# The output projection's last twelve token blocks: seven block products in place of eight, with their sums on GpSimd

## The chip, the cores and the metric

The kernel runs on one core of a Trainium2 chip. The metric is device time in microseconds (us) of one execution; smaller is better. The engines are TensorE (PE, matmuls; PEld is its weight load), VectorE (DVE), ScalarE (ACT), GpSimd (POOL) and SyncE (SP), which here only issues DMA transfers. Each engine works its own queue strictly in program order, so an instruction that waits holds up all that stands behind it on its engine.

## What is computed

A gated mix of two attention blocks over 2048 tokens of width 1024, in float32. Block A is linear attention, block B is softmax attention with 32 heads of width 32; each has its own input projection and output projection:

```python
def reference(A_x, A_wqkv, A_wo, B_x, B_wqkv, B_wo, gate_w):
    x = A_x
    g = _sigmoid((x * gate_w).sum(-1, keepdims=True))
    a = _A_ref(x, A_wqkv, A_wo)        # linear attention, ... @ wo
    b = _B_ref(x, B_wqkv, B_wo)        # softmax attention, o.reshape(B, S, D) @ wo
    return g * a + (1 - g) * b
```

The change touches only the last product, `o @ wo` of block B (2048x1024 by 1024x1024), and what mixes it into the result.

## The kernel before, in words

A float32 product at full speed is made of three matmuls: each operand is written as hi + lo (`split`, L252: ACT rounds the source to fp32r as hi, then DVE or POOL subtracts hi from the source to get lo), and `three` (L144) adds hi·hi, hi·lo and lo·hi in one PSUM bank. The order of all instructions is fixed in Python: a planner keeps a modelled time per engine (`T`, `use`) and picks streams until the attention heads are done. From then on, in `output` (L1252), the order is the plain order of the code.

The output stage goes over 16 blocks of 128 tokens in the order `t_order` (L1157). For a block n:

- `load_o` (L1172) and `load_all` (L1178) fetch it into one tile of the ring `o_ring`: the left half takes the attention output from DRAM, transposed (L1175, k parts 0 to 6, 448 KB; L1188 and L1193 the last k part), the right half takes `ra` (L1176, 512 KB), block A's result for these tokens. A tile is fetched again when the block that used it is done.
- `split_o` (L1195) splits the attention output of a whole block: one ACT cast and one DVE subtraction of 128x1024, into one of four tiles `xo_t`.
- `gate` (L1211) computes g and 1-g from x (two DVE products of 128x512 with a sum, a chain of small DVE and ACT steps) and scales `ra` by g on ACT (L1225); then `load_g` fetches x for the block after next.
- `out_pe` (L1230) runs three matmuls of 128x512 per k part and column half: 8 parts, 2 halves, 48 matmuls per block.
- `out_done` (L1241) evicts a bank on DVE: `ra` becomes (1-g) · bank + `ra` (L1246); then SP stores 256 KB to `out` (L1247).

Blocks 0 and 1 have only their last k part left when the final loop (L1286) begins. PSUM has eight banks, and a block holds two. The loop splits and gates block n+1 ahead of the matmuls of block n, so that PE has a block's time in hand. The weights `wo_t` (hi and lo of 1024x1024) stay in SBUF throughout. POOL has nothing to do in this stage.

The lines that matter elsewhere: `pair_ops` (L379) is an earlier stage in which POOL forms sums of weight tiles (L387 to L392) while DVE runs the subtractions of `split` (L254); L1093 is POOL's running sum in the attention heads, beside which DVE adds to a PSUM bank (L1102).

## Time and profile before

| what | value |
|---|---|
| median of three runs | 2846.59 us (2845.34 to 2848.77) |
| the profiled execution | 2848.47 us, its span 2846.7 us |
| PE busy, share of the span | 2835.8 us, 100% |
| DVE, ACT, POOL busy | 2237.9, 1618.4, 1855.0 us |
| chain that ended last | PE 98%, DMA 1%, DVE 1% |

The profile takes one execution; its span runs from the first to the last instruction, and 1.8 us of the measured time lie around it. Read first the chain that ended last: it names the engine whose work sets the end. Then read the stage in question by itself, since the shares over the whole span mix stages with different limits: the output loop is the last 155 us, and there DVE, ACT and the DMA queues look different from the page's averages. Waits of an engine that is not in the chain cost nothing as long as its results come in time.

### The profile page before, as it was taken

The page shows a single profiled execution, that of the slowest core. Times are in us where ns is not written, and L with a number is a line of the kernel's source. Part 1 is how long each engine was busy: PE and PEld are TensorE (multiplying, and loading weights), DVE is VectorE, ACT ScalarE, POOL GpSimd, SP SyncE. Part 2 cuts the span into 40 slices and gives each one's busy share as a digit, 9 for nine tenths or more (in the row PEclk, how much of TensorE's full clock was granted, in tenths as well). Part 3 has the DMA queues.
Part 4 walks back from the last instruction along what each step waited for, and adds up shares of the span by engine and source line. Part 5 has one row for each costly group of instructions (what it writes and reads, how often), then busy time and mean ns, then how long its engine had stood idle before and what let it go on. Part 6 is the DMA issues. An engine that isn't in the chain of part 4 may idle for free.

```text
span 2846.7 us, 44413 instructions
## 1 busy us (share of the span) xinstructions
PE 2835.8 (100%) x15744; PEld 2034.0 (71%) x15744; DVE 2237.9 (79%) x3775; ACT 1618.4 (57%) x3007; POOL 1855.0 (65%) x646
## 2 busy tenths in 40 slices
PE   9999999999999999999999999999999999999999
PEld 8888888666666666666666767676766666666787
DVE  6666656888888888888888888888988888886743
ACT  5334320666666667666666666675656656666421
POOL 1212220778898889988988888678778787885000
PEclk9999999999999999999999999999999999999999
DMA  5956865432333224233323334564464354424663
GB/s 168 297 167 209 261 193 166 121 97 90 111 90 93 90 80 117 91 103 94 115 83 94 93 119 149 180 219 141 145 191 146 121 148 132 142 88 139 228 216 102
DMA packets 302498, 400.57 MB, mean 141 GB/s; under 512 B 92682, under 2 KB 185354, under 8 KB 299146
## 3 DMA queue, kind: packets, MB, share of 16 engines
q1 hardware_dynamic: 302276, 397.73, 45.1%
q8 instruction: 124, 2.03, 0.3%
q14 instruction: 98, 0.80, 0.1%
HBM read 287.57 MB, written 108.79 MB: 139 GB/s over the span
## 4 chain that ended last, share of the span: by engine, by line
PE 98%; DMA 1%; DVE 1%; ACT 0%; issue 0%; SPq 0%; ACTq 0%
PE bank L1041 17%; PE bank L890 16%; PE bank L1140 15%; PE bank L147 11%; PE bank L149 11%; PE bank L148 11%; PE bank L410 4%; PE bank L408 4%; PE bank L409 4%; PE bank L943 1%; PE bank L447 1%; PE bank L448 1%; PE bank L449 1%; PE bank L693 1%; DMA big<-xs 0%; PE bank L587 0%
## 5 line engine op out<-in xcount | busy, mean ns | idle before, releaser
L1093 POOL TENSOR_TENSOR big<-big,big 128x1536 f32<-128x1536 f32 (+1 forms) x434 | 1557.6, 3589 | 185.1 <-ACT big L1045 162.6
L895 DVE TENSOR_REDUCE mx<-bank 128x1 f32<-128x512 f32 x2048 | 1310.9, 680 | 314.6 <-PE bank L890 310.4
L1045 ACT ACTIVATE big<-bank 128x512 f32<-128x512 f32 x2048 | 1181.7, 602 | 517.7 <-PE bank L1041 450.3
L1041 PE MATMUL bank<-big,big 128*128 128x512 f32 x2048 | 809.7, 397 | 2.5 <-DMA big<-ml 2.4
L890 PE MATMUL bank<-big,big 128*128 128x512 f32 x2048 | 802.7, 392 | 0.3 <-ACT big L1045 0.3
L147 PE MATMUL bank<-big,big 128*128 128x512 f32 x1408 | 551.9, 392 | 1.9 <-DMA big<-xs 1.9
L149 PE MATMUL bank<-big,big 128*128 128x512 f32 x1408 | 550.3, 391 | 0.4 <-DMA big<-xs 0.4
L148 PE MATMUL bank<-big,big 128*128 128x512 f32 x1408 | 550.4, 391 | 0.0
L1041 PEld LDWEIGHTS bank<-big,big 128*128 128x128 f32 x2048 | 383.9, 188 | 158.9 <-issue 64.8
L1140 PE MATMUL bank<-big,mid 128*32 128x512 f32 x4096 | 459.2, 593 | 0.0
L890 PEld LDWEIGHTS bank<-big,big 128*128 128x128 f32 x2048 | 384.6, 188 | 84.8 <-ACT big L1045 4.6
L1140 PEld LDWEIGHTS bank<-big,mid 128*32 128x32 f32 x4096 | 127.7, 110 | 263.7 <-issue 263.7
L147 PEld LDWEIGHTS bank<-big,big 128*128 128x128 f32 x1408 | 264.4, 188 | 65.3 <-ACT big L1045 5.9
L149 PEld LDWEIGHTS bank<-big,big 128*128 128x128 f32 x1408 | 264.4, 188 | 57.1 <-DMA big<-xs 0.9
L148 PEld LDWEIGHTS bank<-big,big 128*128 128x128 f32 x1408 | 264.4, 188 | 55.2
L1102 DVE TENSOR_TENSOR bank<-bank,big 128x512 f32<-128x512 f32 (+1 forms) x434 | 280.4, 646 | 6.9 <-ACT big L1045 5.3
L1089 POOL TENSOR_TENSOR big<-big,big 128x1536 f32<-128x1536 f32 (+1 forms) x31 | 111.6, 3601 | 235.1 <-ACT big L1045 122.1
L254 DVE TENSOR_TENSOR big<-mid,big 128x512 fp32r<-128x512 f32 x216 | 152.9, 731 | 81.1 <-ACT big L253 80.9
L387 POOL TENSOR_TENSOR mid<-mid,mid 128x512 f32<-128x512 f32 x16 | 20.6, 1289 | 277.1 <-DVE big L254 251.2
L253 ACT CAST big<-mid 128x512 fp32r<-128x512 f32 x216 | 130.1, 624 | 93.1 <-POOL mid L388 53.9
L409 PE MATMUL bank<-big,big 128*128 128x512 f32 x448 | 174.3, 389 | 0.0
L410 PE MATMUL bank<-big,big 128*128 128x512 f32 x448 | 174.3, 389 | 0.0
(103 smaller groups left out, 1977.2 us busy)
## 6 DMA issues: line engine op xcount, KB each, us to landing
big<-xs SPq DMA_DIRECT2D x208, 512.0 KB
qk<-mid SPq DMA_DIRECT2D x128, 256.0 KB
big<-oA SPq DMA_DIRECT2D x64, 512.0 KB
big<-qk SPq DMA_DIRECT2D x96, 256.0 KB
big<-qk SPq DMA_DIRECT2D x384, 64.0 KB
mid<-in_b_wqkv SPq DMA_DIRECT2D x88, 256.0 KB
xs<-big SPq DMA_DIRECT2D x64, 256.0 KB
oA<-mid SPq DMA_DIRECT2D x64, 256.0 KB
```

The costliest lines, as they stand in the source:

```text
L147: yield nc.tensor.matmul(ps, sh, mh_, start=(kt == 0), stop=False)
L148: yield nc.tensor.matmul(ps, sh, ml_, start=False, stop=False)
L149: yield nc.tensor.matmul(ps, sl, mh_, start=False, stop=(kt == NK - 1))
L409: nc.tensor.matmul(ps, sh, ml_, start=False, stop=False)
L410: nc.tensor.matmul(ps, sl, mh_, start=False, stop=(i == HK - 1))
L890: nc.tensor.matmul(bank[b], q[:, t * P:(t + 1) * P], k[:, j * C:(j + 1) * C], start=True, stop=True)
L895: nc.vector.tensor_reduce(m[:, t, j:j + 1], bank[b], AX.X, ALU.max)
L1041: nc.tensor.matmul(bank[b], k[:, t * P:(t + 1) * P], q[:, j * C:(j + 1) * C], start=True, stop=True)
L1045: nc.scalar.activation(pr_t[i][:, j * C:(j + 1) * C], bank[b], AF.Exp, scale=SCALE)
L1093: nc.gpsimd.tensor_add(lacc[:, :qp], lacc[:, :qp], pr(t)[:, :qp])
L1102: nc.vector.tensor_add(lacc[:, qp:] if t == NT - 1 else l_b[:, :n], l_b[:, :n], src)
L1140: nc.tensor.matmul(av_b[j * DH:(j + 1) * DH, :], v[:, t, :], pr(t)[:, j * C:(j + 1) * C], start=(t == 0), stop=(t == NT - 1))
```

## The change

The first four blocks stay as they were. The last twelve are taken in six pairs. A pair's 256x1024 attention output and the 1024x1024 weights are both cut into 2x2 quarters, and the eight quarter products (12 matmuls each, 96 for a pair) are replaced by seven products of sums of quarters (Strassen's scheme), 84 matmuls in all. What is added:

- `t_load`, `t_sums`, `t_part`: `wo` is fetched a second time, in 16 tiles of 256 KB (four k rows i, four tiles each); for each i POOL forms four sums or differences in place (128x512) and three of them are split at once (ACT cast, DVE subtraction); the fourth is split after block 2. They stand between the splits and gates of blocks 0 to 3.
- `operand`: the seven stationary operands of a pair. POOL forms four sums in the ring tiles and also the lo parts of operands 2 to 5; ACT casts all seven; DVE subtracts for operands 0, 1 and 6. Operand i of the next pair is queued after product i of this one.
- `pair`: seven products over four banks. Product 0 stays in its bank; product 2 is added to it, then product 4, and the partial sums are evicted after each step: eight evictions for a pair in place of four. The next pair's blocks are fetched by `load_all` when a pair is done, both at once; the ring has four tiles in place of five.

```diff
-        o_ring.extend(pr_t[slot(H - 1, t)] for t in (NT - 5, NT - 3, NT - 2, NT - 1))
+        o_ring.extend(pr_t[slot(H - 1, t)] for t in (NT - 5, NT - 3, NT - 2))
...
+    def t_load(i):
+        for which, (k, c) in enumerate(((i, 0), (i, 1), (HK + i, 0), (HK + i, 1))):
+            nc.sync.dma_start(t_raw(which, i), b_wo[k * P:(k + 1) * P, c * C:(c + 1) * C])
+
+    def t_part(which, i, raw):
+        hi, lo = t_w[which]
+        split(hi[:, i * C:(i + 1) * C], lo[:, i * C:(i + 1) * C], raw, nc.vector)
...
+    def t_sums(i):
+        b11, b12, b21, b22 = [t_raw(w, i) for w in range(4)]
+        nc.gpsimd.tensor_sub(b11, b12, b11)
+        nc.gpsimd.tensor_sub(b12, b22, b12)
+        nc.gpsimd.tensor_sub(b22, b22, b11)
+        nc.gpsimd.tensor_sub(b21, b21, b22)
+        for which, raw in ((0, b11), (2, b12), (1, b22)):
+            t_part(which, i, raw)
+        if i + 2 < HK:
+            t_load(i + 2)
...
+    def operand(p, i):
...
+        src = (a[0], a[1], a[0], s1, a[2], a[1], a[3])[i]
+        if i == 1:
+            nc.gpsimd.tensor_add(s1, a[2], a[3])
+            nc.gpsimd.tensor_sub(a[2], a[0], a[2])
+        elif i == 2:
+            nc.gpsimd.tensor_sub(a[0], s1, a[0])
+            nc.gpsimd.tensor_sub(a[1], a[1], a[0])
+        eng = nc.gpsimd if 2 <= i < 6 else nc.vector
+        split(op_part(p, i, 0), op_part(p, i, 1), src, eng)
...
+    def pair(p):
...
+        plan = ((0, weights[0], True, (0,)), (1, weights[1], True, (0,)), (0, sums[1], False, (1,)),
+                (2, sums[0], True, (3,)), (0, sums[2], False, (2, 3)), (2, weights[2], False, (1,)),
+                (3, sums[3], True, (2,)))
+        for i, (at, w, first, outs) in enumerate(plan):
+            b = banks[at]
...
+            for k in range(HK):
+                for j, (x_, m) in enumerate(((hi, w[k][0]), (hi, w[k][1]), (lo, w[k][0]))):
+                    nc.tensor.matmul(bank[b], x_[:, sl], m, start=(first and k == 0 and j == 0),
+                                     stop=(k == HK - 1 and j == 2), skip_group_check=not first)
...
+            for o in outs:
...
+                nc.vector.scalar_tensor_tensor(ras[t][:, sl], bank[b], omg_sb[:, tok:tok + 1], ras[t][:, sl],
+                                               op0=ALU.mult, op1=ALU.add)
+                if (o, i) in ((0, 1), (3, 4), (1, 5), (2, 6)):
+                    nc.sync.dma_start(out[tok * P:(tok + 1) * P, sl], ras[t][:, sl])
...
+            if p + 1 < NPAIR_O:
+                operand(p + 1, i)
+            if i == 0:
+                gate(n + 1)
+            elif i == 4 and n + 2 < NT:
+                gate(n + 2)
+        o_done[0] += 2
+        load_all()
...
-        for n in range(NT):
-            if 2 < n + 1 < NT and n >= NF:
+        t_load(0)
+        t_load(1)
+        t_sums(0)
+        for n in range(PAIR_FROM):
+            if n == NF:
                 split_o(n + 1, slice(0, NK))
-            if NF <= n + 1 < NT:
+            if NF <= n + 1:
                 gate(n + 1)
+            if n + 1 < HK:
+                t_sums(n + 1)
             for c in range(NQC):
                 for k in range(NK - 1 if n < NF else 0, NK):
                     out_pe(n, c, k)
+                if n == PAIR_FROM - 1:
+                    for i in range(2):
+                        operand(0, 2 * c + i)
                 out_done(n, c)
+            if n == NF:
+                for i in range(HK):
+                    t_part(3, i, t_raw(2, i))
+        for i in range(4, 7):
+            operand(0, i)
+        for p in range(NPAIR_O):
+            pair(p)
```

DVE's queue from block 2's split (into big5) to block 3's, before; L1246 evicts blocks 0 and 1, L1217 to L1223 are the gate of block 2:

```order
L254 TENSOR_TENSOR big5_213<-big6_3750,big5_213 128x1024
L1246 SCALAR_TENSOR_TENSOR big12_3759<-bank2_246,omg_sb_198,big12_3759 128x512
L1246 SCALAR_TENSOR_TENSOR big12_3759<-bank5_249,omg_sb_198,big12_3759 128x512
L1217 SCALAR_TENSOR_TENSOR mid8_237,tg_199<-mid8_237,zrep_196 128x512
L1217 SCALAR_TENSOR_TENSOR mid9_238,tg_199<-mid9_238,zrep_196 128x512
L1219 TENSOR_TENSOR g_sb_197<-tg_199 128x1
L1221 TENSOR_SCALAR g_sb_197<-g_sb_197 128x1
L1222 RECIPROCAL g_sb_197<-g_sb_197 128x1
L1223 TENSOR_SCALAR omg_sb_198<-g_sb_197 128x1
L1246 SCALAR_TENSOR_TENSOR big10_3754<-bank1_245,omg_sb_198,big10_3754 128x512
L1246 SCALAR_TENSOR_TENSOR big10_3754<-bank0_244,omg_sb_198,big10_3754 128x512
L254 TENSOR_TENSOR big20_21417<-big7_3751,big20_21417 128x1024
```

The same queue after the change, from the gate of block 2 (L1218) to the split of block 3, which now goes into big9; ahead of these rows six subtractions L255 (from mid0, mid3, mid5, mid1, mid4, mid6) and block 0's two evictions follow block 2's split:

```order
L1218 SCALAR_TENSOR_TENSOR mid8_237,tg_199<-mid8_237,zrep_196 128x512
L1218 SCALAR_TENSOR_TENSOR mid9_238,tg_199<-mid9_238,zrep_196 128x512
L1220 TENSOR_TENSOR g_sb_197<-tg_199 128x1
L1222 TENSOR_SCALAR g_sb_197<-g_sb_197 128x1
L1223 RECIPROCAL g_sb_197<-g_sb_197 128x1
L1224 TENSOR_SCALAR omg_sb_198<-g_sb_197 128x1
L255 TENSOR_TENSOR big17_225<-mid0_229,big16_224 128x512
L255 TENSOR_TENSOR big19_227<-mid3_232,big18_226 128x512
L255 TENSOR_TENSOR big8_21420<-mid5_234,big20_21419 128x512
L1247 SCALAR_TENSOR_TENSOR big10_3754<-bank1_245,omg_sb_198,big10_3754 128x512
L1247 SCALAR_TENSOR_TENSOR big10_3754<-bank0_244,omg_sb_198,big10_3754 128x512
L255 TENSOR_TENSOR big9_21210<-big7_3751,big9_21210 128x1024
```

So nine subtractions of weight sums, from tiles that POOL writes, now stand ahead of block 3's split on DVE, and the three casts of each step ahead of its cast on ACT.

DVE's queue over one block of the middle of the loop, before: split, gate and two evictions:

```order
L254 TENSOR_TENSOR big9_21210<-big12_3759,big9_21210 128x1024
L1217 SCALAR_TENSOR_TENSOR mid7_236,tg_199<-mid7_236,zrep_196 128x512
L1217 SCALAR_TENSOR_TENSOR mid10_239,tg_199<-mid10_239,zrep_196 128x512
L1219 TENSOR_TENSOR g_sb_197<-tg_199 128x1
L1221 TENSOR_SCALAR g_sb_197<-g_sb_197 128x1
L1222 RECIPROCAL g_sb_197<-g_sb_197 128x1
L1223 TENSOR_SCALAR omg_sb_198<-g_sb_197 128x1
L1246 SCALAR_TENSOR_TENSOR big8_3752<-bank2_246,omg_sb_198,big8_3752 128x512
L1246 SCALAR_TENSOR_TENSOR big8_3752<-bank5_249,omg_sb_198,big8_3752 128x512
L254 TENSOR_TENSOR big5_213<-big10_3754,big5_213 128x1024
```

The same queue after the change, in the third pair from the eviction of product 0 to that of product 2 (L1332; big12 and big10 are the pair's ring tiles, big6 and big7 the next pair's, L255 the subtractions of operands 0 and 1 of the next pair):

```order
L1332 SCALAR_TENSOR_TENSOR big12_3759<-bank5_249,omg_sb_198,big12_3759 128x512
L255 TENSOR_TENSOR mid4_21632<-big6_3750,mid3_21631 128x512
L1218 SCALAR_TENSOR_TENSOR mid7_236,tg_199<-mid7_236,zrep_196 128x512
L1218 SCALAR_TENSOR_TENSOR mid10_239,tg_199<-mid10_239,zrep_196 128x512
L1220 TENSOR_TENSOR g_sb_197<-tg_199 128x1
L1222 TENSOR_SCALAR g_sb_197<-g_sb_197 128x1
L1223 RECIPROCAL g_sb_197<-g_sb_197 128x1
L1224 TENSOR_SCALAR omg_sb_198<-g_sb_197 128x1
L1332 SCALAR_TENSOR_TENSOR big12_3759<-bank2_246,omg_sb_198,big12_3759 128x512
L255 TENSOR_TENSOR mid6_21664<-big6_3750,mid5_21663 128x512
L1332 SCALAR_TENSOR_TENSOR big12_3759<-bank5_249,omg_sb_198,big12_3759 128x512
```

The eviction of product 2 now stands behind operand 1's subtraction, which needs the whole left half of the next pair's first ring tile.

SP's queue at the end of a block, before: two stores, then the block's four loads and x for a later gate:

```order
L1247 DMA out_0<-big6_3750 128x512 x2
L1175 DMA big6_3750<-oB_127 128x896
L1176 DMA big6_3750<-ra13_183 128x1024
L1188 DMA big6_3750<-oB_127 96x128
L1193 DMA big6_3750<-mid11_240 32x128
L1209 DMA mid8_237<-in_x 128x512
L1209 DMA mid9_238<-in_x 128x512
```

The same queue after the change, at the end of the third pair:

```order
L1335 DMA out_0<-big12_3759 128x512
L1335 DMA out_0<-big10_3754 128x512
L1176 DMA big12_3759<-oB_127 128x896
L1177 DMA big12_3759<-ra3_173 128x1024
L1176 DMA big10_3754<-oB_127 128x896
L1177 DMA big10_3754<-ra7_177 128x1024
L1189 DMA big12_3759<-oB_127 96x128
L1189 DMA big10_3754<-oB_127 96x128
L1194 DMA big12_3759<-mid11_240 32x128
L1194 DMA big10_3754<-mid11_240 32x128
L1210 DMA mid7_236<-in_x 128x512
L1210 DMA mid10_239<-in_x 128x512
```

The last k part of the next pair's first block (L1189, L1194) now follows the large loads of both its blocks.

## Rows read from the trace of the kernel before

**Rows 1.** The page: busy time by engine, and the chain that ended last.
```profile
PE 2835.8 (100%) x15744; PEld 2034.0 (71%) x15744; DVE 2237.9 (79%) x3775; ACT 1618.4 (57%) x3007; POOL 1855.0 (65%) x646
...
PE 98%; DMA 1%; DVE 1%; ACT 0%; issue 0%; SPq 0%; ACTq 0%
```
**Rows 2.** Windows of 20 us: busy by engine, granted clock, DMA share, GB/s.
```profile
2700.00:2720.00 20.00, 20.00 (x90) 16.57 (x89) 8.97 (x22) 4.81 (x7) 0.00 (x0) 1.00 0.85 275
...
2780.00:2800.00 20.00, 20.00 (x90) 16.57 (x89) 7.21 (x21) 4.59 (x6) 0.00 (x0) 1.00 0.63 196
```
**Rows 3.** Timeline of PE, output loop: start, length, line, tiles.
```profile
2687.64 0.39 PE L147 MATMUL bank<-big,big 128*128 128x512 f32 x1
...
2842.23 0.39 PE L148 MATMUL bank<-big,big 128*128 128x512 f32 x1
2842.45 0.39 PE L149 MATMUL bank<-big,big 128*128 128x512 f32 x1
```
**Rows 4.** Groups by line, last 247 us: count | busy us, mean ns | idle before.
```profile
L1246 DVE SCALAR_TENSOR_TENSOR big<-bank,omg_sb,big 128x512 f32<-128x512 f32 x32 | 23.8, 749 | 84.1 <-PE bank L149 84.1
...
L1225 ACT ACTIVATE big<-big,g_sb 128x1024 f32<-128x1024 f32 x16 | 18.4, 1152 | 6.7 <-DVE g_sb L1222 6.7
L254 DVE TENSOR_TENSOR big<-big,big 128x1024 fp32r<-128x1024 f32 x14 | 17.0, 1216 | 1.3 <-ACT big L253 1.3
...
L254 DVE TENSOR_TENSOR big<-mid,big 128x512 fp32r<-128x512 f32 x16 | 10.6, 688 | 11.4 <-ACT big L253 11.4
L253 ACT CAST big<-mid 128x512 fp32r<-128x512 f32 x16 | 10.2, 664 | 2.7 <-DVE big L1106 2.7
```
**Rows 5.** Groups by line on POOL, whole span: sums of 128x512.
```profile
L387 POOL TENSOR_TENSOR mid<-mid,mid 128x512 f32<-128x512 f32 x16 | 20.6, 1289 | 277.1 <-DVE big L254 251.2 <-DMA qk<-mid 25.9
```
**Rows 6.** Timeline of POOL in an early stage: sums of weight tiles.
```profile
53.44 1.29 POOL L392 TENSOR_TENSOR mid<-mid,mid 128x512 f32<-128x512 f32 x1 [0.63 <-DVE big L254]
60.58 1.29 POOL L387 TENSOR_TENSOR mid<-mid,mid 128x512 f32<-128x512 f32 x1 [5.86 <-DVE big L254]
61.95 1.61 POOL L388 TENSOR_TENSOR mid<-mid,mid 128x512 f32<-128x512 f32 x1
```
**Rows 7.** Timeline of DVE in the same stage: lo subtractions of 128x512.
```profile
48.13 0.69 DVE L254 TENSOR_TENSOR big<-mid,big 128x512 fp32r<-128x512 f32 x1
...
53.74 1.54 DVE L254 TENSOR_TENSOR big<-mid,big 128x512 fp32r<-128x512 f32 x1 [0.38 <-ACT big L253]
...
61.02 1.40 DVE L254 TENSOR_TENSOR big<-mid,big 128x512 fp32r<-128x512 f32 x1
```
**Rows 8.** Groups by line on DVE: additions into a bank beside POOL's running sums.
```profile
L1102 DVE TENSOR_TENSOR bank<-bank,big 128x512 f32<-128x512 f32 x364 | 250.8, 689 | 5.6 <-ACT big L1045 4.3
```
**Rows 9.** Timeline of DVE around the start of the output loop.
```profile
2681.20 0.69 DVE L1217 SCALAR_TENSOR_TENSOR mid<-mid,zrep 128x512 f32<-128x512 f32 x1 [6.17 <-DMA mid<-in_x]
...
2690.57 0.68 DVE L1217 SCALAR_TENSOR_TENSOR mid<-mid,zrep 128x512 f32<-128x512 f32 x1
...
2692.72 0.15 DVE L1223 TENSOR_SCALAR omg_sb<-g_sb 128x1 f32<-128x1 f32 x1
```
**Rows 10.** Timeline of SP's queue: x for blocks 2 and 3; a store, then loads.
```profile
2684.33 2.98 SPq L1209 DMA_DIRECT2D mid<-in_x  x4
...
2734.86 0.34 SPq L1247 DMA_DIRECT2D out<-big  x1
...
2737.35 0.33 SPq L1176 DMA_DIRECT2D big<-ra  x1
```
**Rows 11.** A window in which the DMA engines are all busy.
```profile
2674.00:2676.00 2.00, 2.00 (x10) 1.65 (x10) 0.99 (x2) 0.00 (x0) 0.00 (x0) 1.00 0.99 374
```
**Rows 12.** Timeline of PE at the start of the kernel.
```profile
6.34 0.63 PE L448 MATMUL bank<-big,big 128*128 128x512 f32 x1
...
9.75 0.63 PE L447 MATMUL bank<-big,big 128*128 128x512 f32 x1
...
10.75 0.39 PE L447 MATMUL bank<-big,big 128*128 128x512 f32 x1
```

More of the change, by code (lines that the diff above doesn't have):

```diff
@@ L40 @@
 WO_STEP = 4
+PAIR_FROM = 4
 LATE = 1.0
@@ L1250, in out_done, with t_raw @@
             load_all()
+    t_w = []
+    def t_raw(which, i):
+        return mid[((0, 1)[i % 2], (3, 4)[i % 2], (2, 12, 13, 14)[i], (5, 6)[i % 2])[which]]
+    def t_load(i):
[4 more added lines that the diff above has]
+        split(hi[:, i * C:(i + 1) * C], lo[:, i * C:(i + 1) * C], raw, nc.vector)
+        use("dve", 0.73, use("act", 0.62))
@@ new lines, in t_sums, with op_part @@
+    def t_sums(i):
[8 more added lines that the diff above has]
+            t_load(i + 2)
+    NPAIR_O = (NT - PAIR_FROM) // 2
+    op_mid = {}
+    def op_part(p, i, part):
+        at = (7 * p + i) % 10
+        if at < 4:
+            m = ((0, 1), (3, 4), (5, 6), (2, 12))[at][part]
+            if m not in op_mid:
+                op_mid[m] = sb.tile([P, C], F32R, name=f"mid{m}")
+            return op_mid[m]
+        if at < 6:
+            o = ((at - 4) * 2 + part) * C
+            return xo_t[1][:, o:o + C]
+        return wo_part(at - 6, part)[:, C:]
@@ new lines, in operand @@
+    def operand(p, i):
+        n = PAIR_FROM + 2 * p
+        a = [o_ring[(n + t) % len(o_ring)][:, h * C:(h + 1) * C] for t in range(2) for h in range(2)]
+        s1 = mid[(13, 14)[p % 2]]
+        src = (a[0], a[1], a[0], s1, a[2], a[1], a[3])[i]
[7 more added lines that the diff above has]
+        split(op_part(p, i, 0), op_part(p, i, 1), src, eng)
+        use("act", 0.62)
@@ L1281, in output @@
         RING.extend((4, 7))
-        xo_t[3] = big_tile(LACC[(H - 1) % 2], F32R)
+        xo_t[3] = xo_t[1]
         split_o(0, KL)
```

17 lines of the change are left out of this document (added).

## The prediction, made before the result was known

> **What bounds the kernel now.** I read the busy times and the chain that ended last first: PE is busy for the whole span and makes 98% of the chain [rows 1], so a matmul less is worth its time, if nothing else becomes late. Then the windows of the output loop, which is where the change sits: PE is busy 20.00 of 20 us, DVE only 7 to 9, ACT under 5, POOL 0 [rows 2]. There the cover looks wide. PE's own timeline gives the price: the final loop has 684 matmuls, the first starting at 2687.64 and the last at 2842.45 [rows 3], so 154.81 / 683 = 0.2267 us each. After the last one come an eviction and a store, as before and after the change.
>
> **What is removed.** Six pairs run 84 matmuls in place of 96. 72 x 0.2267 = 16.3 us, all of it on the bounding engine. This is the most that the change can bring, 0.57%.
>
> **What is added on other engines, in sum.** For a pair (19.0 us of PE): DVE 8 evictions of 0.75 [rows 4], 3 subtractions of 0.69 [rows 4] and two gates of 2.15 (2690.57 to 2692.72 [rows 9]), 12.4 us; POOL 8 sums of 1.29 [rows 5], 10.3 us; ACT 7 casts of 0.66 and two scalings of 1.15 [rows 4], 7.0 us. Each fits into 19.0. So no engine becomes the bound by its sum; what counts is the order in the queues, and one row that the sums don't show.
>
> **That row.** In an early stage POOL also sums weight tiles beside DVE's subtractions. A subtraction with POOL idle takes 0.69. One that starts at 53.74, while POOL works from 53.44 to 54.73, takes 1.54 and ends at 55.28, which is 0.55 after POOL's end [rows 6, 7]. Another, from 61.02, ends at 62.42, again 0.55 after POOL's end at 61.87; and POOL's next sum, from 61.95, takes 1.61 in place of 1.29 [rows 6, 7]. So these two take turns: from POOL's end at 61.87 to its next end at 63.56 is 1.69, 0.40 more than a sum alone. Additions with one operand in a PSUM bank keep 0.689 beside POOL [rows 8]; evictions are of that kind. The subtractions added here read two SBUF tiles, as in [rows 7], and so do the gate's two products; no row shows those beside POOL, and I price them by [rows 7], the nearest, with no extra cost as the other end. The Trainium skill, page "SBUF — State Buffer", section "Who interferes with whom", states it as a rule: a DVE instruction with two SBUF inputs and a GpSimd instruction that reads SBUF lock each other out, and whichever comes second waits for the whole of the first. By that rule the gates would pay too, which is the end that I take from the rows anyway.
>
> **Term A, entry to block 3.** Block 2's split stands ahead of the new work; block 3's stands behind the splits of three of the four weight steps. When do the weight tiles land? Before, x for blocks 2 and 3 left SP from 2684.33 to 2687.31 [rows 10], after the gates of blocks 0 and 1, which had waited for their own x until 2681.20 [rows 9]. With one ring tile less, about 1.0 MB (block 3's loads) now goes behind that x; at 374 GB/s [rows 11] that is 2.7 us earlier. So x is out by 2684.6, the first two weight tiles leave by 2685.1, and with 2.5 us for a transfer (a 256 KB store leaves at 2734.86, and the load that waits for it at 2737.35 [rows 10]) POOL starts at 2687.5; 2686.5 to 2690 are the bounds. PE would reach block 3 at 2687.64 + 60 x 0.2267 = 2701.2, and needs its lo part two matmuls later, 2701.7.
> Without turns: seven sums 9.0, cast and subtraction 1.35, two evictions 1.5, gate 2.15, scaling 1.15, cast 0.66, three subtractions 2.1, two evictions 1.5, block 3's own subtraction 1.2 [rows 4, 5, 9]: 20.6, so 2708.1, and PE waits 6.4.
> With turns: POOL is then never idle through its 16 sums, and 11 DVE instructions (nine subtractions, the gate's two products) fall among them: 16 x 1.29 + 11 x 0.40 = 25.0; then a subtraction 0.55, two evictions 1.5, the split 1.2: 28.3, so 2715.8, and PE waits 14.1. I take this.
>
> **Term B, entry to pair 0.** From the end of block 3's split DVE and ACT have to go through gate 2.15, scaling 1.15, cast 0.66, three subtractions 2.1, two evictions 1.5, four subtractions 2.8, gate 2.15, scaling 1.15, cast 0.66 and operand 0's subtraction 0.69: 15.0 us. PE has 48 matmuls until it needs that, 10.9. It waits 4.1, and 4.5 with two meetings with POOL.
>
> **Term C, inside pair 0.** Product 2 is added to product 0's bank, and product 4 to the same: each waits for an eviction. In pair 0 the eviction of product 0 stands behind operand 6's subtraction, whose cast stands behind those that need POOL's two late sums (2 x 1.69, casts 1.3 after that, a subtraction in turn, an eviction): about 6.6 after operand 0's subtraction, where product 2 is due after 5.0. Wait 1.6. From there operand 0 of the next pair 1.1, gate 3.2 with its turns, scaling 1.15, cast 0.66, subtraction in turn 1.85, eviction 0.75: 8.7, where product 4 is due 5.4 to 5.7 later. Wait 3.0. Sum 4.6; without turns 0.7.
>
> **Term D, the later pairs.** Operands of a pair come from loads that leave when the pair before last is done. Counted from that pair's last matmul: eviction 1.0, store out at 1.2, then 448, 512, 448, 512 and 96 KB; with the store 2.3 MB, at 374 GB/s 6.2 us [rows 11], and some 2 us for the first to come [rows 10]: the last k part lands at 9.5, and at 10.4 if the gate's turns delay the last but one eviction and its store. Operand 1 needs it: cast 0.66, subtraction 0.69, then the eviction of product 2, 0.75, for which product 4 waits, due at 10.9. Without turns 11.7, a wait of 0.8; with turns the subtraction also meets POOL's first sum, which starts on the same landing: 13.3, a wait of 2.4. Four boundaries, the first milder since pair 0 is stretched: 1.3 + 3 x 2.4 = 8.5 (3.2 without turns). Every us by which the landing is off counts four times.
>
> **Sum.** Waits 14.1 + 4.5 + 4.6 + 8.5 = 31.7, less 16.3: 15.4 us slower. On the profiled execution: span 2846.7 + 15.4 = 2862.1, and 2863.9 with the 1.8 us around it. That execution took 2848.47, 1.9 above the median of 2846.59; on the median the forecast is 2862.
>
> **Rivals.**
> First, no turns in this stage: the waits are 6.4 + 4.1 + 0.7 + 3.2 = 14.4, and the change is 1.9 us faster, 2845. For it speaks that the sums fit easily and that ACT's casts often hold the subtractions anyway; against it [rows 6, 7], same instruction, same shapes. It decides from where a meeting costs under about 0.2 in place of 0.4 us: then no more than 5.7 us are left. I give it 0.15.
> Second, turns for the subtractions but not for the gates: term A loses 2.2, C 1.9, D 3.3, so 8 us slower, 2854.6. Nothing but the lack of a row speaks for it: 0.12.
> Third, the clock. In the first microseconds of the kernel matmuls start 0.426 apart (nine from 6.34 to 9.75) and then 0.23, from about 10.5 on [rows 12]: the 1.2 and the 2.4 GHz level; in the output loop the granted clock stands at 1.00 [rows 2]. PE idles for most of 14 us ahead of block 3. If the clock falls there, ten to twenty matmuls lose 0.2 each, 2 to 4 us, but these run against term B's wait and cost little. If it falls again at the waits of pair 0 and of each pair, 4 x 2 us come on top: 2870. 0.13. The Trainium skill, page "TensorE: Matmul & The Clock Gate", Part 1, says that the half rate is what the engine returns to when it is idle, which would bring the first fall here; no row of the kernel before has such a gap.
> That the change doesn't do what it says can be left out: the new order has 612 matmuls in the final loop, 72 fewer.
>
> **How the numbers follow.** The forecast, turns throughout, has 0.60. The range goes from 2846, which leaves out the larger part of the first rival, to 2870, which takes in the landing's bounds (1 us, four times) and the third. A change of 0.2%, 5.7 us, is about what a measurement of this kernel can tell. Slower by more: the forecast, the second and the third nearly whole, 0.80. Within: most of the first and some of the second, 0.14. Faster: a first rival with early landings, 0.06.
>
> **What would show it.** PE's matmuls still 0.2267 apart in the pairs; an idle PE of 14 us (two matmuls in between) ahead of block 3, ended by ACT's cast and DVE's subtraction of its split; 4.5 us ahead of pair 0; 2.4 us ahead of product 4 in the later pairs, ended by a DVE eviction. Subtractions of 1.1 to 1.5 us where POOL is at work, and sums of 1.6. It is wrong if subtractions keep 0.69 beside POOL, if the weight tiles land before 2686, or if the wait ahead of block 3 is under 7 us.

## The result, and the profile after

The changed kernel takes 2880.74 us in the median of four runs (2876.95 to 2883.67), the kernel before 2846.32 in the same session: a ratio of 1.0119, 95% interval 1.0101 to 1.0136, or 34 us slower. The direction was forecast, the size was not: 15 us were expected, and the time lies 11 us above the upper end of the range. The profiled execution, the slowest of the four, took 2883.67 us with a span of 2881.8.

The page of the changed kernel, busy times and the chain that ended last (as [rows 1]):

```profile
PE 2831.7 (98%) x15672; PEld 2025.4 (70%) x15672; DVE 2285.1 (79%) x3821; ACT 1637.1 (57%) x3053; POOL 1944.5 (67%) x710
...
PE 93%; DMA 3%; DVE 2%; issue 1%; ACT 1%; SPq 0%; POOL 0%; ACTq 0%; DVEq 0%; POOLq 0%
```

PE still makes the chain, but no longer alone: 98% have become 93%. Its matmuls in the final loop, with each wait and what ended it (start, duration, engine, line, operation, tiles, count, idle time before):

```profile
2687.86 0.39 PE L148 MATMUL bank<-big,big 128*128 128x512 f32 x1
...
2701.23 0.39 PE L150 MATMUL bank<-big,big 128*128 128x512 f32 x1
2715.02 0.79 PE L148 MATMUL bank<-big,big 128*128 128x512 f32 x1 [13.40 <-ACT big L254]
...
2719.63 0.80 PE L150 MATMUL bank<-big,big 128*128 128x512 f32 x1 [3.39 <-DVE big L255]
2720.22 0.63 PE L148 MATMUL bank<-big,big 128*128 128x512 f32 x1
2720.65 0.63 PE L149 MATMUL bank<-big,big 128*128 128x512 f32 x1
...
2734.78 6.01 PE L1324 MATMUL bank<-big,mid 128*128 128x512 f32 x24 [2.65 <-ACT mid L254]
2742.43 5.71 PE L1324 MATMUL bank<-big,mid 128*128 128x512 f32 x24 [1.65 <-DVE big L1332]
2751.71 11.85 PE L1324 MATMUL bank<-big,big 128*128 128x512 f32 x39 [3.57 <-DVE big L1332]
...
2775.56 8.41 PE L1324 MATMUL bank<-big,mid 128*128 128x512 f32 x36 [1.80 <-DVE big L1332]
...
2799.84 8.31 PE L1324 MATMUL bank<-big,big 128*128 128x512 f32 x24 [4.99 <-DVE big L1332]
...
2824.11 9.80 PE L1324 MATMUL bank<-big,big 128*128 128x512 f32 x42 [2.37 <-DVE big L1332]
...
2848.17 8.05 PE L1324 MATMUL bank<-big,mid 128*128 128x512 f32 x24 [4.74 <-DVE big L1332]
...
2872.38 5.60 PE L1324 MATMUL bank<-big,mid 128*128 128x512 f32 x24
```

Read the brackets first. They hold nine waits, each at a place that the prediction named: 13.40 and 3.39 ahead of block 3, 2.65 ahead of pair 0, 1.65 and 3.57 ahead of its products 2 and 4, and 1.80, 4.99, 2.37, 4.74 ahead of product 4 of pairs 1 to 4. Together they are 38.6 us. Then read the durations: 24 matmuls at 0.2267 take 5.6 us with the last one's tail, as in the last row; behind the waits of 4.99 and 4.74 they take 8.31 and 8.05, and block 3's first matmuls start 0.43 apart. The windows show the clock there (PE, PEld, DVE, ACT, POOL busy, then the granted clock, DMA share and GB/s), which stood at 1.00 before [rows 2]:

```profile
2700.00:2720.00 20.00, 3.21 (x11) 1.87 (x10) 17.53 (x20) 5.34 (x9) 15.95 (x11) 0.66 0.61 195
2720.00:2730.00 10.00, 10.00 (x38) 8.07 (x38) 8.09 (x20) 4.99 (x9) 1.56 (x1) 0.83 0.80 257
2750.00:2760.00 10.00, 8.29 (x25) 6.62 (x25) 4.77 (x10) 1.74 (x4) 4.98 (x4) 0.66 0.13 46
...
2800.00:2810.00 10.00, 10.00 (x33) 8.01 (x34) 4.26 (x12) 3.05 (x6) 6.44 (x6) 0.73 0.21 69
```

A window between the levels of 1.2 and 2.4 GHz has spent part of its time on the lower one. Against 0.2267 per matmul this costs 0.6 us behind the first of block 3's waits and 1.9 behind the second, and 2.85, 2.7 and 2.45 at the waits ahead of product 4 of pairs 0, 2 and 4: 10.5. The 6.01 of pair 0's first 24 matmuls is not the clock: 0.4 of it is a wait of the third matmul for operand 0's lo part. The account closes: waits 38.6, lower clock 10.5, that 0.4, 1.5 for nine tails (a wait is counted from 0.39 after the last matmul's start, not 0.2267), less 16.3 for the 72 matmuls, is 34.7; the spans differ by 35.1.

### The profile page after: what moved, and what is told of

Read it like the earlier page. It is cut to its first block, busy times and chain, and to the rows that moved or that the text cites. A ratio compares the mean times of both kernels' runs of the same rounds, so it can differ in the third digit from the quotient of the medians.

```text
span 2881.8 us, 44552 instructions
## 1 busy us (share of the span) xinstructions
PE 2831.7 (98%) x15672; PEld 2025.4 (70%) x15672; DVE 2285.1 (79%) x3821; ACT 1637.1 (57%) x3053; POOL 1944.5 (67%) x710
## 4 chain that ended last, share of the span: by engine, by line
PE 93%; DMA 3%; DVE 2%; issue 1%; ACT 1%; SPq 0%; POOL 0%; ACTq 0%; DVEq 0%; POOLq 0%
PE bank L1042 17%; PE bank L891 16%; PE bank L1141 15%; PE bank L148 9%; PE bank L150 9%; PE bank L149 9%; PE bank L411 4%; PE bank L409 4%; PE bank L410 4%; PE bank L1324 3%; PE bank L944 1%; PE bank L448 1%; PE bank L449 1%; PE bank L450 1%; DVE mid L1218 1%
## 5 line engine op out<-in xcount | busy, mean ns | idle before, releaser
L1042 PE MATMUL bank<-big,big 128*128 128x512 f32 x2048 | 809.6, 397 | 3.5 <-DMA big<-ml 2.4
L891 PE MATMUL bank<-big,big 128*128 128x512 f32 x2048 | 802.6, 392 | 0.2 <-ACT big L1046 0.2
L1042 PEld LDWEIGHTS bank<-big,big 128*128 128x128 f32 x2048 | 383.8, 188 | 160.4 <-issue 64.9
L148 PE MATMUL bank<-big,big 128*128 128x512 f32 x1216 | 478.1, 393 | 15.5 <-ACT big L254 13.4
L150 PE MATMUL bank<-big,big 128*128 128x512 f32 x1216 | 476.6, 392 | 3.9 <-DVE big L255 3.4
L149 PE MATMUL bank<-big,big 128*128 128x512 f32 x1216 | 476.3, 392 | 0.0
L891 PEld LDWEIGHTS bank<-big,big 128*128 128x128 f32 x2048 | 384.7, 188 | 84.8 <-ACT big L1046 4.5
L148 PEld LDWEIGHTS bank<-big,big 128*128 128x128 f32 x1216 | 228.8, 188 | 71.8 <-ACT big L254 13.8
L150 PEld LDWEIGHTS bank<-big,big 128*128 128x128 f32 x1216 | 229.0, 188 | 53.7 <-DVE big L255 4.5
L149 PEld LDWEIGHTS bank<-big,big 128*128 128x128 f32 x1216 | 228.9, 188 | 47.7
L255 DVE TENSOR_TENSOR big<-mid,big 128x512 fp32r<-128x512 f32 x232 | 170.5, 760 | 88.6 <-ACT big L254 88.0
L388 POOL TENSOR_TENSOR mid<-mid,mid 128x512 f32<-128x512 f32 x16 | 20.6, 1290 | 275.0 <-DVE big L255 250.4
L254 ACT CAST big<-mid 128x512 fp32r<-128x512 f32 x235 | 141.1, 624 | 103.8 <-POOL mid L389 54.4
L409 PE MATMUL bank<-big,big 128*128 128x512 f32 x448 | 174.3, 389 | 0.0
L411 PE MATMUL bank<-big,big 128*128 128x512 f32 x448 | 174.3, 389 | 0.0
```

What stands on the lines that cost most here:

```text
L148: yield nc.tensor.matmul(ps, sh, mh_, start=(kt == 0), stop=False)
L149: yield nc.tensor.matmul(ps, sh, ml_, start=False, stop=False)
L150: yield nc.tensor.matmul(ps, sl, mh_, start=False, stop=(kt == NK - 1))
L409: nc.tensor.matmul(ps, sh, mh_, start=(i == 0), stop=False)
L411: nc.tensor.matmul(ps, sl, mh_, start=False, stop=(i == HK - 1))
L891: nc.tensor.matmul(bank[b], q[:, t * P:(t + 1) * P], k[:, j * C:(j + 1) * C], start=True, stop=True)
```

## The experiments

Times are given against the kernel before of the same session, with the 95% interval of the ratio; 0.1% is 2.8 us. Each trace is one execution, and executions of one kernel differ (e1 takes 2857.90 to 2865.05), so a single wait can differ by 2 us between two traces without any cause in the edit.

| kernel | ratio | interval | us against before |
|---|---|---|---|
| the change | 1.0119 | 1.0101 to 1.0136 | +34 |
| e1 left halves early | 1.0048 | 1.0033 to 1.0062 | +14 |
| e2 weight sums on DVE | 1.0083 | 1.0068 to 1.0098 | +24 |
| e3 waits filled with matmuls | 1.0105 | 1.0089 to 1.0122 | +30 |
| e4 = e1, gate later | 1.0045 | 1.0030 to 1.0060 | +13 |
| e5 = e1, pairs from block 6 on | 1.0010 | 1.0001 to 1.0019 | +3 |
| e6 = e5, sums on DVE, gate later | 0.9992 | 0.9983 to 1.0001 | -2 |
| e7 = e1 + e2, gate later | 1.0024 | 1.0014 to 1.0034 | +7 |
| e8 = e6, entry reordered | 0.9995 | 0.9986 to 1.0004 | -1 |
| e9 weights issued first | 1.0100 | 1.0086 to 1.0114 | +28 |
| e10 = e8, three moves | 0.9986 | 0.9977 to 0.9995 | -4 |
| e11 = e10, entry by due time | 0.9985 | 0.9976 to 0.9994 | -4 |
| e12 = e11, order and filling | 0.9993 | 0.9984 to 1.0002 | -2 |

**When the loads leave (e1).** The left half of a ring tile is last read by operand 6, which is queued a pair ahead; its reload need not wait for the pair's stores. (With four ring tiles, what is loaded at the end of pair p are the blocks of pair p+2.) `load_left` issues the three loads of the attention output, `LEFT_AT` is 2.

```diff
+            if i == LEFT_AT:
+                for m in range(n + 4, min(n + 6, NT)):
+                    load_left(m)
-        o_done[0] += 2
-        load_all()
+        for m in range(n + 4, min(n + 6, NT)):
+            nc.sync.dma_start(o_ring[m % len(o_ring)][:, D:2 * D], ra_d[t_order[m]])
```

> The change, with one thing moved: the left halves (attention output) of the blocks of pair p+2 are fetched behind product 2 of pair p, some 14 us earlier than now; only the 512 KB of ra that wait for the stores still leave at the end of the pair. Theory L (late landing): the waits ahead of product 4 of pairs 1 to 4 (1.80, 4.99, 2.37, 4.74 us in the changed kernel, 13.9 in sum) hang on operands whose loads leave late, so all four fall under 0.5 us, and with them the two stretches at the lower clock behind the 5 us waits (24 matmuls in 8.31 and 8.05 in place of 5.6, 5.2 in sum): 17 to 19 us less, 2862 to 2864 us. Rival Q (the order in DVE's queue and the turns with POOL hold the eviction of product 2, landing or not): half of the waits or more stay, 2872 or above.

The kernel takes 20 us less than the change. PE's rows at product 4 of pairs 0 to 4 in this kernel:

```profile
2746.39 9.12 PE L1332 MATMUL bank<-big,big 128*128 128x512 f32 x39 [3.60 <-DVE big L1340]
...
2766.12 8.41 PE L1332 MATMUL bank<-big,mid 128*128 128x512 f32 x36 [0.42 <-ACT big L254]
...
2785.65 5.71 PE L1332 MATMUL bank<-big,big 128*128 128x512 f32 x24 [0.23 <-ACT big L254]
...
2805.21 9.78 PE L1332 MATMUL bank<-big,big 128*128 128x512 f32 x42 [0.26 <-ACT mid L254]
...
2824.77 5.73 PE L1332 MATMUL bank<-big,mid 128*128 128x512 f32 x24 [0.26 <-ACT big L254]
```

The four waits of 13.9 us are 1.2 now, and 24 matmuls take 5.7 again. DVE's order is unchanged and the turns are still there (a gate's product takes 1.76 at 2779.78), so theory L holds: the landing caused those waits, and the turns alone fit into a pair.

**Turns at the entry (e2).** The four lines of `t_sums`, of which one is shown, go to another engine.

```diff
-        nc.gpsimd.tensor_sub(b11, b12, b11)
+        nc.vector.tensor_sub(b11, b12, b11)
...
```

> The change, with the 16 sums of weight tiles on DVE in place of POOL, in the same places of the order; nothing else moves. DVE gets 16 x 0.69 = 11.0 us more work. Theory T (turns): from the first sum to the end of block 3's split it now takes 28.3 us (2691.30 to 2719.58), of which POOL's sums and the turns are the chain. On DVE alone the same stretch is 12 sums and 9 subtractions of 0.69 = 14.5, two blocks' evictions 3.0, gate 2.2, split 1.2, about 21 to 22: the wait ahead of block 3 falls by 6 to 7, that ahead of pair 0 stays about the same, total 2873 to 2876 us. Rival (DVE is simply overbooked there, POOL's sums run beside it at no cost): with 12 sums more ahead of block 3's split on DVE it ends 8 us later, total 2886 to 2890.

The kernel takes 10 us less than the change, with 11 us more work on DVE. From DVE in this kernel, the first sum, the three subtractions behind the fourth and block 3's split:

```profile
2689.48 0.69 DVE L1269 TENSOR_TENSOR mid<-mid,mid 128x512 f32<-128x512 f32 x1 [2.96 <-DMA mid<-in_b_wo]
...
2692.86 1.89 DVE L255 TENSOR_TENSOR big<-mid,big 128x512 fp32r<-128x512 f32 x3
...
2708.71 1.21 DVE L255 TENSOR_TENSOR big<-big,big 128x1024 fp32r<-128x1024 f32 x1
```

2689.48 to 2709.92 is 20.4 us where the change needs 28.3. So the rival falls. But e2 takes away two things at once, the turns and POOL's slower sum (1.29 for 0.69), and no run parts them; that there are turns is read from rows of the change. The same three subtractions take 5.17 there, and POOL's 16 sums 23.9 in place of 16 x 1.29 = 20.6. Here are POOL, DVE, and again DVE with the gate of block 2, in the changed kernel:

```profile
2691.30 1.29 POOL L1269 TENSOR_TENSOR mid<-mid,mid 128x512 f32<-128x512 f32 x1 [84.68 <-DMA mid<-in_b_wo]
...
2696.28 1.62 POOL L1272 TENSOR_TENSOR mid<-mid,mid 128x512 f32<-128x512 f32 x1
2697.86 1.73 POOL L1269 TENSOR_TENSOR mid<-mid,mid 128x512 f32<-128x512 f32 x1
```

```profile
2693.27 5.17 DVE L255 TENSOR_TENSOR big<-mid,big 128x512 fp32r<-128x512 f32 x3 [4.49 <-ACT big L254]
...
2706.10 1.77 DVE L1218 SCALAR_TENSOR_TENSOR mid<-mid,zrep 128x512 f32<-128x512 f32 x1
...
2709.58 1.09 DVE L1220 TENSOR_TENSOR g_sb<-tg 128x1 f32<-128x1 f32 x1
...
2718.37 1.21 DVE L255 TENSOR_TENSOR big<-big,big 128x1024 fp32r<-128x1024 f32 x1
```

The gate's products wait for POOL as well (1.77 in place of 0.69), and so does its addition of two 128x1 columns (1.09 in place of 0.16). So the prediction's second rival falls.

**The clock (e3).** Matmuls into an idle bank, which nobody reads, ahead of the products that wait.

```diff
+            idle_pe({2: {0: 7}, 4: {0: 15, 1: 8, 2: 21, 3: 10, 4: 20}}.get(i, {}).get(p, 0) if (p, i) != (0, 0) else 20)
             for k in range(HK):
...
+            if n == PAIR_FROM - 1:
+                idle_pe(74)
```

> The change, with matmuls that nobody reads put into PE's waits so that PE is busy in them: 74 ahead of block 3 (0.2267 each, 16.8 us), 20 ahead of pair 0, 7 and 15 ahead of products 2 and 4 of pair 0, 8, 21, 10 and 20 ahead of product 4 of pairs 1 to 4. They end about when the waits end. Theory C (clock): the slow stretches behind the waits (24 matmuls in 8.3 in place of 5.6) come from PE having idled; with PE busy every matmul starts 0.227 behind the one before, the 2.85 + 2.7 + 2.45 = 8.0 us behind the products 4 of pairs 0, 2 and 4 are given back, and the 2.0 behind block 3 turn into a longer wait ahead of pair 0: 2872 to 2874 us. Rival (those matmuls are slow because something else takes their operands' memory, or the weights' sums lie badly): the spacing stays 0.35 to 0.43 there and the time 2880 or more.

With PE busy the clock stays up: the granted clock is 1.00 in each of the windows shown above, and 24 matmuls take 5.67 us.

```profile
2792.73 4.92 PE L1259 MATMUL bank<-big 128*128 128x512 f32 x21
2797.49 5.67 PE L1333 MATMUL bank<-big,big 128*128 128x512 f32 x24
...
2816.59 2.43 PE L1259 MATMUL bank<-big 128*128 128x512 f32 x10
2821.22 9.77 PE L1333 MATMUL bank<-big,big 128*128 128x512 f32 x42 [2.19 <-DVE big L1341]
```

So theory C holds for the cause. For the price it does not: 4 us less by the ratios (whose intervals overlap), 5.6 by the spans, where 8 were expected. The last row tells where the rest went: the next wait is longer, 2.3 us of filling and 2.19 more in place of 2.37, since it hangs on loads and DVE, and a PE that arrives earlier waits longer.

**Where the first sum starts (e9).** The x loads of blocks 2 and 3, which `gate` issued, go behind the first eight weight tiles on SP.

```diff
         t_load(0)
         t_load(1)
+        for n in range(NF, 2 * NF):
+            load_g(n)
```

> The change, with one move: the x loads of blocks 2 and 3 are issued behind the first eight weight tiles instead of ahead of them. In the traces so far POOL's first sum starts 4.9 to 5.5 us after the first weight tile is issued (5.15 in the changed kernel, 2686.15 to 2691.30), and the x loads in front of it take SP 3.5 us. Theory I (the issue on SP, behind x that waits for the gates, sets when the weight tiles land): the weights are issued 3.5 us earlier, POOL starts that much earlier against PE's loop, the idle time ahead of block 3 (13.4 + 3.4) falls by 3 to 4 us and the total by 2 to 4, 1.0105 to 1.0112 of before. Rival B (the landing is bound by the bytes in flight, over 2 MB of block and x loads in front): POOL starts less than 1.5 us earlier, the total within 1 us of the change's.

The change's SP rows, then those of e9, with POOL's first sum and block 3's first matmul of e9:

```profile
2682.65 3.45 SPq L1210 DMA_DIRECT2D mid<-in_x  x4
2686.15 3.79 SPq L1260 DMA_DIRECT2D mid<-in_b_wo  x8
```

```profile
2679.99 5.64 SPq L1260 DMA_DIRECT2D mid<-in_b_wo  x8
2685.72 1.96 SPq L1210 DMA_DIRECT2D mid<-in_x  x4
```

```profile
2684.57 1.29 POOL L1269 TENSOR_TENSOR mid<-mid,mid 128x512 f32<-128x512 f32 x1 [78.39 <-DMA mid<-in_b_wo]
```

```profile
2707.60 0.80 PE L148 MATMUL bank<-big,big 128*128 128x512 f32 x1 [6.40 <-ACT big L254]
```

The sums start 4.6 us after the first weight tile is issued (5.15 in the change), so with the issue they move forward; PE's wait falls from 13.40 to 6.40 and the total by 5 us, where 2 to 4 were expected. Theory I holds. Some of the 7.0 is the spread of single executions: in e1 and e4, whose entry is that of the change, this wait is 11.16 and 13.41.

**What is left (e4 to e8, e10 to e12).** e4 moves `gate(n + 1)` of `pair` from behind product 0 to behind product 2.

```diff
-            if i == 0:
+            if i == 2:
                 gate(n + 1)
```

> The first experiment's kernel (left halves fetched early), with the gate of a pair's second block moved in the order from behind product 0 to behind product 2. What is left of term C there is one wait, 3.60 us ahead of product 4 of pair 0, ended by an eviction on DVE. Theory G (the gate, 3 us with its turns, stands ahead of the eviction of product 2 in DVE's queue): the wait falls under 1 us, 2.6 to 3.6 us less than the first experiment, about 2860. Rival S (the eviction is held by the subtractions that need POOL's late sums for operands 1 and 2, and the gate only fills their wait): it stays above 2.5, 2863.

The 3.60 ahead of product 4 is gone, but 1.96 at product 5 has come in its place, and the time is e1's within the intervals. The 1.65 of the change ahead of product 2 is there too; in e1's trace it is not, because the lower clock stretches products 0 and 1 there (48 matmuls in 13.33 for 11.0). So theory G has the place right and the gain wrong: the gate's work on DVE now holds a later eviction. e5 to e7 ask whether cover or turns were lacking. In e5 and e6 the weights also go ahead of x, as in e9, and the splits of blocks 3 to 5 ahead of the sums.

```diff
-PAIR_FROM = 4
+PAIR_FROM = 6
...
+        block(1)
+        split_block(3)
+        gate(2)
+        t_sums(0)
+        gate(3)
+        t_sums(1)
+        block(2)
+        split_block(4)
...
```

> Blocks 4 and 5 stay as they were, pairs from block 6 on: five pairs, 60 matmuls saved, 13.6 us. The weight sums stay on POOL with all their turns, but have the time of blocks 2 to 5 (44 us of PE) to hide behind instead of blocks 2 and 3, and each block's split stands ahead of them; left halves are fetched early as in the first experiment. Theory P (the loss at the entry is lack of cover: about 45 us of DVE and POOL work in front of pair 0 against 24 us of PE): the 13.4 + 3.4 + 2.65 us of waits ahead of block 3 and pair 0 nearly vanish (under 4 in sum), product 4 of pair 0 keeps its 3.6, the later pairs their 0.3 each: 13.6 less 7 to 8, so 5 to 7 us faster than before, 2842 to 2845 where before takes 2849.6. Rival (turns stretch whatever stands beside them, and with more blocks beside the sums more is stretched): waits of 10 us or more stay, 2847 or above.

> As the kernel with pairs from block 6 on, with the 16 weight sums on DVE (0.69 each, no turns in the entry) and the gate behind product 2. DVE then has in one block's 10.9 us: two evictions 1.5, split 1.2, gate 2.2, four sums and three subtractions 4.8 = 9.7, so it just fits. Theory T: no wait above 1 us ahead of blocks 3 to 5 and pair 0, product 4 of pair 0 under 1: 13.6 less 2 to 3, 2838 to 2840, and 3 to 5 us less than with the sums on POOL. Rival (with this cover the turns hide as well): no difference between the two.

> The change with six pairs as it is, and all three remedies: left halves early, weight sums on DVE, gate behind product 2. If the three add up (20.2 and 10.9 us measured for the first two alone, 3 expected of the third), the 34 us that the change lost against the kernel before are gone: 2849 to 2852, within 0.1% of before. If they hide behind each other (pair 0 then waits for what is left), 2855 or more.

Two more plain blocks, the weights ahead of x and the earlier splits together bring 11 us over e1 (+14 to +3); e9 brought 5 with the weights alone, and no run parts the rest. In e5 waits of 11.2 us stay, within the number that its rival gave. Sums on DVE with the later gate bring another 5, as theory T had it, and in e6 waits of 6.3 us are left, in pair 0 above all. e7 shows that the remedies add up to 27 of the 31 us that e1 and e2 brought singly. Against before, none of e5 to e8 reached its expected time: e5 and e6 missed it by 9 and 8 us, e7 and e8 by at least 4. e8 and e10 to e12 then chase what is left: each is aimed at the wait that the trace of the one before shows in pair 0.

e8 puts a slot's sums ahead of its gate, and operand 0 and the fourth split earlier:

```diff
-        gate(4)
         t_sums(2)
+        gate(4)
         block(3)
...
+        operand(0, 0)
         block(4)
-        gate(6)
```

> The kernel with pairs from block 6 on, weight sums on DVE, early left halves and the gate behind product 2, with the entry put into another order: the weight sums of a step stand ahead of the gate of the same slot and its x loads behind theirs, operand 0 of pair 0 ahead of block 4's evictions, the fourth sum's split right behind block 4, the gate of pair 0's first block behind operand 1. In the kernel it comes from, pair 0 lost 0.91 + 1.39 ahead of and inside product 0, 1.22 ahead of product 2, 1.95 ahead of product 5 and 1.8 to a lower clock, 7.3 us, because the fourth split and POOL's sums behind it ran 6 us late (DVE stood 2.5 us for x of block 4, then 2 us for casts behind a gate). Theory P (these all hang on that one delay): under 2 us of the 7.3 stay, so 4 to 6 us less: 2840 to 2843 where before takes 2848. Rival N (POOL's eight operations of pair 0 and the turns with DVE's subtractions set the pace of pair 0 by themselves): waits ahead of products 2 and 5 stay, 1 to 2 us less only, 2844 to 2846.

In e8 pair 0 waits 4.69 ahead of product 2 and 2.46 ahead of product 5, the places that rival N named, and the time is e6's. e10 has pair 0's token sums on DVE, operand 6 ahead of operand 2, and both gates of a pair in the pair before; block 5's evictions now stand behind gates 6 and 7 on DVE:

```diff
+        add = nc.gpsimd if p else nc.vector
...
+            if i in (4, 5) and n + i - 2 < NT:
+                gate(n + i - 2)
...
+        for i in (1, 6, 2):
+            operand(0, i)
+        gate(6)
+        gate(7)
```

> The reordered kernel with pairs from block 6 on, which still lost 4.69 us ahead of product 2 and 2.46 ahead of product 5 of pair 0, and 1.7 to a lower clock. In its trace the eviction of product 0 stands on DVE behind operand 6's subtraction, whose cast stands on ACT behind those that need POOL's sums; the eviction ahead of product 5 stands behind a gate of 6.4 us (two products with turns, the scaling). Three moves: operand 6 ahead of operand 2 for pair 0; pair 0's four token sums on DVE (0.69 in place of 1.3 to 1.7, POOL keeps the lo parts); both gates of a pair in the pair before, behind products 4 and 5. Theory E (these evictions alone hold PE): the waits in pair 0 fall under 1.5 us in sum and no slow stretch is left, total 2837 to 2840, 0.25 to 0.4% under before. Rival M (the next engine in line, ACT with its casts or POOL with its four lo parts of 1.3, holds the operands themselves): 3 us or more of waits remain, now ended by an ACT cast or a POOL subtraction, 2841 to 2845.

e11 orders the entry by due time:

```diff
+        t_part(3, 2, t_raw(2, 2))
+        for i in range(3):
+            operand(0, i)
+        gate(5)
+        gate(6)
...
+            if i == 0 and p == 0:
+                for c in range(NQC):
+                    out_done(5, c)
+                gate(7)
```

> As the kernel before it (pairs from block 6 on), which had one wait left worth naming: 6.09 us ahead of product 4 of pair 0, ended by ACT's cast of operand 4, and 1.9 to a lower clock behind it. That cast stood on ACT behind the scalings of two gates. Here the entry's DVE work is put by due time: token sums of operands 1 and 2 first, gates 5 and 6 behind them, block 4's evictions and the rest of the fourth split next, block 5's evictions and the gate of pair 0's second block behind product 0's eviction. Theory E (order alone): DVE's work up to product 0's eviction fits, waits in pair 0 under 2 us in sum, 5 to 6 us less: 2838 to 2840, 0.3 to 0.4% under before. Rival W (the work in front of pair 0 is more than DVE can do in the 44 us of blocks 2 to 5, whatever its order): 4 us or more of waits come back in another place of pair 0, and the total stays within 2 us, 2842 to 2845.

e12 moves casts ahead of gate 6 and fills one wait:

```diff
+        for i in (2, 0, 1, 3):
+            t_part(3, i, t_raw(2, i))
+        operand(0, 0)
+        gate(5)
+        for i in (1, 2, 3):
+            operand(0, i)
+        gate(6)
...
+            if (p, i) == (0, 2):
+                idle_pe(9)
```

> The entry once more, on the kernel before it, which lost 4.64 us ahead of product 2 and 1.22 ahead of product 5 of pair 0, and 3.0 to a lower clock (24 matmuls in 8.60 in place of 5.6). Two edits: all casts of the fourth split and of operands 0 to 3 stand ahead of gate 6 on ACT, so that DVE no longer waits 1.5 us for them behind two scalings; and nine matmuls that nobody reads (9 x 0.2267 = 2.0 us) stand ahead of product 2 of pair 0. Theory C + E: the wait shrinks to about 2 us beside the filling or less, the clock stays at its upper level in pair 0 (24 matmuls in 5.7), 4 to 6 us less: 2839 to 2841, 0.3% under before. Rival W (DVE's overload only shows in another place): waits of 4 us or more behind the filling or ahead of later products, and no gain, 2843 to 2846.

The longest wait of pair 0 in e8, e10, e11 and e12, one row each:

```profile
2743.97 7.30 PE L1335 MATMUL bank<-big,mid 128*128 128x512 f32 x24 [4.69 <-DVE big L1343]
```

```profile
2745.32 8.12 PE L1336 MATMUL bank<-big,mid 128*128 128x512 f32 x24 [6.09 <-ACT big L254]
```

```profile
2743.61 8.60 PE L1336 MATMUL bank<-big,mid 128*128 128x512 f32 x24 [4.64 <-DVE big L1344]
```

```profile
2752.24 11.36 PE L1345 MATMUL bank<-big,big 128*128 128x512 f32 x39 [5.11 <-DVE big L1353]
```

By PE's order (12 matmuls a product) these waits stand ahead of product 2 in e8, e10 and e11 and ahead of product 4 in e12; the expectation of e11 put e10's ahead of product 4, and that of e12 put e11's 1.22 ahead of product 5 where it stands ahead of product 4. The row of e10 names operand 4's cast, but product 2 adds to product 0's bank, and that eviction ended only 0.15 before it, late behind the two gates and block 5's evictions:

```profile
2744.43 0.74 DVE L1344 SCALAR_TENSOR_TENSOR big<-bank,omg_sb,big 128x512 f32<-128x512 f32 x1
```

So e10's time is rival M's, but by the program its cause is the late eviction. In e12 the filled place keeps the clock up (24 matmuls in 5.72 behind the filling), and 5.11 comes ahead of product 4. The wait moves and keeps some 5 us, and the times are those of rival W of e11 and e12. In e11 DVE is busy 12.18 of the 13 us ahead of pair 0 (the third busy figure of the row, behind PE's and PEld's), which leaves little room:

```profile
2720.00:2733.00 13.00, 13.00 (x59) 10.78 (x58) 12.18 (x18) 4.67 (x8) 1.69 (x1) 1.00 0.67 231
```

That no other order would fit is not shown. e10 and e11 beat both kernels. Against before it is 4 us or 0.15%, a third of the 13.6 us that five pairs save, and the intervals end at 0.9995 and 0.9994.

## Why the prediction went wrong, step by step

Three steps failed: the start of POOL's sums in term A, the landing of the loads in term D, and the clock, which the sum put at nothing. The waits stood where they were forecast.

- **What is removed.** This was right: there are 612 matmuls, 0.2267 apart wherever PE neither waited nor ran at the lower clock.
- **Turns.** They were right, in size too. From POOL's first sum to the end of block 3's split 28.3 us were forecast and 28.3 measured (2691.30 to 2719.58). That it agrees to the tenth is luck: POOL also waited 0.6 for a load, and the gate's addition waited for POOL, neither of which the sum had. Subtractions and gates both pay, as the rows of L255 and L1218 above show. The Trainium skill's page "SBUF — State Buffer", section "Who interferes with whom", has the second of two such instructions wait for the whole of the first; this case's rows agree, 1.77 for the gate's product that ends at 2707.87, 0.55 after POOL's end.
- **Term A.** The wait was 16.8 us (13.40 + 3.39) for 14.1: the chain was right, its start was not. "So x is out by 2684.6" and "POOL starts at 2687.5" failed; x was out at 2686.10, and POOL started at 2691.30, outside the bounds. Taking block 3's 1.0 MB out of the queue ahead of x did not bring x 2.7 us earlier: the first gate began at 2680.65, where it was 2681.20 [rows 9]. And the 2.5 us for a transfer, read from one store [rows 10], are 5.15 from the issue of the first weight tile to the sum that needs the first two (4.6 to 5.5 in e1, e3, e4, e9). The megabyte of x in front is not the main reason, since e9 has 4.6 without it.
- **Term B.** The chain was nearly right: from the end of block 3's split to the end of operand 0's subtraction it took 15.9 us (2719.58 to 2735.45, the first of the two in this row) for 15.0. The wait is 2.65, and 0.4 more for the lo part, for 4.5, because block 3 ran 1.9 us longer at the lower clock, as the third rival said of its first fall.

```profile
2734.76 1.29 DVE L255 TENSOR_TENSOR mid<-big,mid 128x512 fp32r<-128x512 f32 x2 [1.54 <-ACT mid L254]
```

- **Term C.** The waits were right, 1.65 and 3.57 for 1.6 and 3.0, the second in part by luck: the gate took 5.4 us (2743.23 to 2748.59) for 3.2, with both products and the addition waiting for POOL, and the subtraction behind it 0.69 for 1.85, since it met no sum.
- **Term D.** The waits were 13.9 us for 8.5. The mechanism is the one forecast; the landing was mis-sized in two pairs of four. These rows show SP, ACT and DVE at the boundary of pairs 1 and 2; pair 1's last matmul ends at 2783.97 (2775.56 + 8.41):

```profile
2785.05 1.00 SPq L1335 DMA_DIRECT2D out<-big  x2
2786.14 0.41 SPq L1176 DMA_DIRECT2D big<-oB  x1
...
2790.06 1.28 SPq L1194 DMA_DIRECT2D big<-mid  x2
```

```profile
2790.52 0.62 ACT L254 CAST mid<-big 128x512 fp32r<-128x512 f32 x1 [4.13 <-DMA big<-oB]
...
2796.95 0.62 ACT L254 CAST mid<-big 128x512 fp32r<-128x512 f32 x1 [1.80 <-DMA big<-mid]
```

```profile
2781.59 1.76 DVE L1218 SCALAR_TENSOR_TENSOR mid<-mid,zrep 128x512 f32<-128x512 f32 x1
2784.28 1.40 DVE L1332 SCALAR_TENSOR_TENSOR big<-bank,omg_sb,big 128x512 f32<-128x512 f32 x2
...
2798.95 1.40 DVE L1332 SCALAR_TENSOR_TENSOR big<-bank,omg_sb,big 128x512 f32<-128x512 f32 x2
```

  The gate behind product 4 meets POOL, so products 5 and 6 are evicted together, the first load leaves 2.2 us after the pair in place of 1.2, and the last k part lets ACT go on at 2796.95, 13.0 after the pair's end: the forecast had 10.4 with the delayed store. The rate was mis-sized: from 2786 to 2797 the DMA engines moved 303 GB/s at a share of 0.93, for 374 [rows 11], and 2.3 MB take 1.4 us longer at that. After a pair that a long wait and the lower clock stretched, the gate meets no POOL work (0.68, 0.69 at 2806.66), the first load leaves 1.2 us after the pair (2812.12), and the next wait is short: 1.80, 4.99, 2.37, 4.74. "Every us by which the landing is off counts four times" stood in the prediction; its range took 1 us for it, and it was 2.6 and 2.3.
- **The clock.** It stood at 0.13 as a rival: one fall at block 3 that costs little, and 2 us at each of four later waits. It fell at block 3 (2.5 us, of which term B's wait took 1.9 back) and at product 4 of pairs 0, 2 and 4 (8.0 us). e3 prices all of it at 4 to 6, as the rest hides behind waits that follow. It should not have been a rival but a term, since no row showed a clock that stays up through such a wait. The Trainium skill's page "TensorE: Matmul & The Clock Gate", Part 1, says that the engine goes back to half rate when it idles; the granted clock of 0.66 in two windows above agrees with that.
- **The sum.** Of the 19 us that are missing, term A is 2.7, D 5.4, C 0.6, tails 1.5, lower clock 10.5, the lo part 0.4, less 1.9 at B. The range reached to 2870 because D's landing and the clock were taken one by one; they came together: two of the four falls stand at the very waits that D's landing made longer.

## What to carry to other kernels

Fewer matmuls pay only if the engines that prepare their operands have time in hand, and that is counted in queue order with turns and landings, not by busy shares: here 16 us saved on PE met 50 us of waits and lower clock. Where the waits stood on an engine that was nearly full, reordering only moved them (e8 to e12); take work off such an engine, or give it more cover, and start loads when the last reader is done rather than when the whole buffer is. Count a PE wait with what the clock loses behind it.
